# Sliding-window attention with a gated MLP on one core: the attention stages ordered in runs of two row blocks

## The chip, the core and the metric

The kernel runs on one core of a Trainium2 chip. The metric is the device time of one execution, in microseconds. A core has five engines that run their own programs and meet at semaphores: TensorE (PE in the profile; matmuls into PSUM), VectorE (DVE), ScalarE (ACT), GpSimd (POOL) and SyncE (SP, which here only issues DMAs). DMAs can be issued from SP, ACT and POOL; POOL's are listed in the profile as "software_dynamic", the others as "hardware_dynamic".

## What is computed

The reference, cut to what matters. S = 2048 rows, D = 640, 32 heads of 192, the last W = 512 keys of the cache, F = 1536:

```python
xn = layernorm(x)
q = (xn @ wq) per head
scores = q @ k[last 512].T * 192 ** -0.5
p = softmax(scores)
s = (p @ v[last 512], heads side by side) @ wo
h = sigmoid(xn @ w_gate) * (xn @ w_up)
g = silu(h @ w_down)
return x + s * g
```

## The kernel before

The program is in two parts. The first (lines 175 to 362) normalises x, turns it (`xnT`, and `xnS` with its partition halves swapped) and computes the gate `g` for all rows, which goes to DRAM as `gB_d`. It also loads the first head group's keys, values and query weights from POOL's queue and has SP turn the keys by DMA transposes (`turn_k`).

The second part is the attention, from line 365 on. Heads are taken in pairs, two pairs make a group (G = 2), so there are NG = 8 groups. Rows are taken in NST = 4 blocks of 512, of four tiles of 128. A block `n` is one (group, row block); there are 32, all four row blocks of a group after each other. For each block TensorE has four kinds of stage:

- `stage_q` (L409), three per block, the query projection: 20 matmuls on halves of the array, listed as 64*128 in the profile. DVE copies the result to `qT` (L414).
- `stage_s` (L425), eight per block, the scores: 12 matmuls of the form 64*128. ACT takes the exponential into `E` (L429).
- `stage_pv` (L441), four per block, the product with the values: 16 matmuls on the whole array (128*128). DVE takes the reciprocal of the row sums and writes `o_st` (L447, L448); after every second one SP turns `o_st` into `oT` by a DMA transpose (L454).
- `stage_wo` (L486), four per block, one per tile of 128 rows, the output projection: 12 matmuls of the form 128*128 on the `oT` of both head pairs. DVE adds it to `acc` (L525); the first group copies it (L523).

The order is written out by hand. In block n all scores come first, with the query stages of block n + 1 between them (SSQ SSQ SSQ SS). Then each of the four value stages is followed by an output stage of block n - 1. Every stage takes the next of four PSUM bank pairs (`bank2`), so a stage starts when the reader of the stage four before it is done. Each engine executes its own instructions in program order.

Weights, keys and values of the next group are loaded while this one is worked on. `load_ahead` issues them from ACT's queue: query weights and keys of one head pair in each of the group's first two blocks, values in the third (with the key transposes on SP), output weights `wo_g` in the last. The query weights, turned keys, values and output weights have two buffers each. `o_st` has two tiles.

In group 6 `prep_last` multiplies `acc` by the gate and adds x, on POOL, tile by tile, with POOL loading gate and x. In group 7 `finish` multiplies the projection by the gate on DVE (L496) and adds `acc`: on DVE, but for the last two blocks on POOL (L497). SP sends the tile out (L498). `load_gate` (L459) issues the gate loads from POOL.

Of the kernel before, what the change touches and what calls it, by code (L numbers as in the profile page):

```python
# [9 lines left out]
ALU = mybir.AluOpType  # L10
BF16 = mybir.dt.bfloat16
F32 = mybir.dt.float32
# [3 lines left out]
def kernel(  # L16
# [13 lines left out]
    nc = tc.nc  # L30
    P = 128
# [4 lines left out]
    S, D = xf.shape  # L36
# [8 lines left out]
    KC = W // P  # L45
    assert S % 512 == 0
    NST = S // 512
    TQ = 4
# [5 lines left out]
    G = 2  # L54
    NG = NPAIR // G
    NWARM = (9, 2)
    FA = 3
    PC = 3
# [29 lines left out]
    gB_d = dram.tile([S, D], BF16, name="gB_d")  # L88

    rs = dict(side="right")  # L90
    xnt_pool = ctx.enter_context(tc.tile_pool(name="xnt_pool", bufs=1, **rs))
    wq_pool = ctx.enter_context(tc.tile_pool(name="wq_pool", bufs=2, **rs))
    k_pool = ctx.enter_context(tc.tile_pool(name="k_pool", bufs=2, **rs))
    kt_pool = ctx.enter_context(tc.tile_pool(name="kt_pool", bufs=2 * G, **rs))
    v_pool = ctx.enter_context(tc.tile_pool(name="v_pool", bufs=1, **rs))

    HF = 64
# [3 lines left out]
    xnS = [xnt_pool.tile([P, NCD, 512], BF16, name=f"xnS{s}") for s in range(NST)]  # L101
    xnT = [xnt_pool.tile([P, NCD, 512], BF16, name=f"xnT{s}") for s in range(NST)]

    NV = 4 * G
    v_tiles = []
    for i in range(NV):
        vt = v_pool.tile([P, KC, DH + 2], BF16, name=f"v_sb{i}")
# [7 lines left out]

    k_of = {}

    def load_k(hp, eng):

        k_sb = k_pool.tile([P, KC * PC, 2, HF], BF16, name="k_sb")  # L120
        for i in range(2):
            hk = (2 * hp + i) // rep
            eng.dma_start(
                k_sb[:, :, i, :],
                A_k_cache[0, hk, Sk - W:Sk, :].rearrange("(p k) (j e) -> p (k j) e", k=KC, j=PC),
            )
        k_of[hp] = k_sb

    def load_v(hp, eng):
        v_t[hp] = []  # L130
        for i in range(2):
            hk = (2 * hp + i) // rep
            vt = v_tiles[(2 * hp + i) % NV]
            eng.dma_start(
                vt[:, :, 0:DH],
                A_v_cache[0, hk, Sk - W:Sk, :].rearrange("(p j) d -> p j d", j=KC),
            )
            v_t[hp].append(vt)

    def load_wq(hp, eng):  # L140


        if hp % G == 0:
            wq_t[hp // G] = wq_pool.tile([P, G * PC // 2, NCD * 2, 2, HF], BF16, name="wqp")
        wqp = wq_t[hp // G]
        for j in range(PC):
            jj = (hp % G) * PC + j
            r = HI if jj % 2 else LO
            for i in range(2):
                d0 = (2 * hp + i) * DH + j * HF  # L150
                eng.dma_start(
                    wqp[r, jj // 2, :, i, :],
                    wq_r[:, :, :, d0:d0 + HF].rearrange("p c h n -> p (c h) n"),
                )

    def turn_k(hp):
        kT = kt_pool.tile([P, KC * PC, P], BF16, name="kT")
        nc.sync.dma_start_transpose(kT[:], k_of[hp][:].rearrange("p k i e -> p (k i e)"))
        kT_t[hp] = kT


    with ExitStack() as bctx:
# [147 lines left out]
        for s in range(NST):  # L310
# [40 lines left out]
            nc.sync.dma_start(xnS[s][HI], xnT[s][LO])  # L351
            if s == 0:
                for hp in range(G):
                    load_k(hp, nc.gpsimd)
                for hp in range(G):
                    load_v(hp, nc.gpsimd)
                    load_wq(hp, nc.gpsimd)
            elif s == 1:
                for hp in range(G):
                    turn_k(hp)  # L360


    acc_pool = ctx.enter_context(tc.tile_pool(name="acc_pool", bufs=1))
    wo_pool = ctx.enter_context(tc.tile_pool(name="wo_pool", bufs=2))
    qT_pool = ctx.enter_context(tc.tile_pool(name="qT_pool", bufs=2))
    e_pool = ctx.enter_context(tc.tile_pool(name="e_pool", bufs=2))
    ost_pool = ctx.enter_context(tc.tile_pool(name="ost_pool", bufs=2))
    oT_pool = ctx.enter_context(tc.tile_pool(name="oT_pool", bufs=2 * G))
    small = ctx.enter_context(tc.tile_pool(name="small", bufs=8))
    fin = ctx.enter_context(tc.tile_pool(name="fin", bufs=2))  # L370
    fout = ctx.enter_context(tc.tile_pool(name="fout", bufs=4))
    gate_pool = ctx.enter_context(tc.tile_pool(name="gate_pool", bufs=TQ + 1))

    acc = [acc_pool.tile([P, D], F32, name=f"acc{t}") for t in range(NST * TQ)]
    wo_t = {}

    def load_wo(g, eng):
        wo_g = wo_pool.tile([P, G * PC, D], BF16, name="wo_g")
        eng.dma_start(wo_g[:], wo_r[:, g * G * PC:(g + 1) * G * PC, :])
        wo_t[g] = wo_g  # L380

    def load_ahead(g, s):


        if s < G:
            load_wq(g * G + s, nc.scalar)
            load_k(g * G + s, nc.scalar)
        elif s == G:
            for hp in range(g * G, (g + 1) * G):
                load_v(hp, nc.scalar)  # L390
                turn_k(hp)
        if s == NST - 1:
            load_wo(g, nc.scalar)

# [2 lines left out]
    def stage_q(n, u):  # L399

        g, s = blocks[n]
        if u == 0:
            qT_t[n] = qT_pool.tile([P, G * PC, 512], BF16, name="qT")
        ps = bank2()
        for c in range(NCD):
            for h in range(2):
                for b, r in enumerate((LO, HI)):
                    x = xnT if b == h else xnS
                    nc.tensor.matmul(  # L409
                        ps[:, b, :], lhsT=wq_t[g][r, u, 2 * c + h].rearrange("p i e -> p (i e)"),  # L410
                        rhs=x[s][r, c, :],
                        start=(c == 0 and h == 0), stop=(c == NCD - 1 and h == 1),
                    )
        nc.vector.tensor_copy(qT_t[n][:, 2 * u:2 * u + 2, :], ps)  # L414
# [39 lines left out]
            nc.sync.dma_start_transpose(oT[:], o_st[:].rearrange("p q d -> p (q d)"))  # L454
            oT_t[n, pp] = oT

    def load_gate(t):
        gB_sb = gate_pool.tile([P, D], BF16, name="gBa_sb")
        nc.gpsimd.dma_start(gB_sb[:], gB_d[t * P:(t + 1) * P, :])  # L459
        return gB_sb  # L460

    prep_in = {}

    def prep_load(t):
        gB_sb = load_gate(t)
        x_sb = fin.tile([P, D], BF16, name="xa_sb")
        nc.gpsimd.dma_start(x_sb[:], xf[t * P:(t + 1) * P, :])
        prep_in[t] = gB_sb, x_sb
# [20 lines left out]
                    start=(cc == 0), stop=(cc == nn - 1),  # L489
                )  # L490

    def finish(ps, gB_sb, t, d0, d1, add):
        t_sb = fin.tile([P, D], F32, name="t_sb")
        o_sb = fout.tile([P, D], BF16, name="o_sb")
        d = slice(d0, d1)
        nc.vector.tensor_tensor(t_sb[:, d], ps, gB_sb[:, d], ALU.mult)  # L496
        add.tensor_tensor(o_sb[:, d], t_sb[:, d], acc[t][:, d], ALU.add)  # L497
        nc.sync.dma_start(of[t * P:(t + 1) * P, d], o_sb[:, d])  # L498

    gates = {}  # L500

    def stage_wo(n, q):
        g, s = blocks[n]
        t = s * TQ + q
        if g == NG - 1:

            for tt in range(t, min(t + 4, NST * TQ)):
                if tt not in gates:
                    gates[tt] = load_gate(tt)
            gB_sb = gates[t]  # L510
        if n == last and q == TQ - 1:

            ps, h = bank2(), D // 2
            for i in range(2):
                wo_mm(ps[:, i, :], n, q, [(i * h, h)], i * h)
                finish(ps[:, i, 0:h], gB_sb, t, i * h, (i + 1) * h, nc.vector)
            return
        oA = flat(bank2())
        wo_mm(oA, n, q, d_chunks)
        if g == NG - 1:  # L520
            finish(oA[:, 0:D], gB_sb, t, 0, D, nc.gpsimd if n >= last - 1 else nc.vector)
        elif g == 0:
            nc.vector.tensor_copy(acc[t][:], oA[:, 0:D])  # L523
        else:
            nc.vector.tensor_tensor(acc[t][:], oA[:, 0:D], acc[t][:], ALU.add)  # L525
        if g == NG - 2:
            prep_last(t)

    blocks = [(g, s) for g in range(NG) for s in range(NST)]
    last = len(blocks) - 1  # L530
    qT_t, E_t, oT_t, ost_t = {}, {}, {}, {}
    load_wo(0, nc.gpsimd)
    for u in range(G * PC // 2):
        stage_q(0, u)
    for n, (g, s) in enumerate(blocks):

        todo = [(pp, c) for pp in range(G) for c in range(KC)]
        for k, (pp, c) in enumerate(todo):
            stage_s(n, pp, c)
            if k % 2 == 1 and k // 2 < G * PC // 2 and n < last:  # L540
                stage_q(n + 1, k // 2)
        if g + 1 < NG:
            load_ahead(g + 1, s)

        pv = [(n, pp, i) for pp in range(G) for i in range(2)]
        wo = [(n - 1, q) for q in range(TQ)] if n > 0 else []
        if n < last:
            for k, u in enumerate(pv):
                stage_pv(*u)
                if wo:  # L550
                    stage_wo(*wo[k])
        else:
            for k, u in enumerate(pv):
                stage_pv(*u)
                if k == 1:
                    stage_wo(*wo.pop(0))
            for u in wo:
                stage_wo(*u)
    for q in range(TQ):
        stage_wo(last, q)  # L560

# [28 lines left out]
```

The softmax here doesn't subtract the row's maximum and nothing guards it: scores larger than these inputs give would overflow.

## Time and profile before

| | us |
|---|---|
| median of 5 runs (lowest, highest) | 937.99 (937.67, 938.34) |
| the profiled execution | 937.75 |
| its span, first to last instruction | 936.0 |
| start of the first value stage (L441) | 182.89 |
| last matmul starts | 927.3 |

The mean granted TensorE clock is 0.997. The page shows busy time by engine, groups of instructions with their mean duration, and what ended the idle time before them. Lines of it that bear on the order of the work:

```profile
L429 ACT ACTIVATE E<-ps_all 128x1024 bf16<-128x1024 f32 x256 | 247.8, 1022 | 496.2 <-PE ps_all L425 443.6
L486 PE MATMUL ps_all<-wo_g,oT 128*128 128x512 bf16 (+2 forms) x1536 | 228.2, 299 | 0.0
L441 PE MATMUL ps_all<-v_sb,E 128*128 128x193 bf16 x2048 | 194.6, 247 | 0.1
L448 DVE TENSOR_TENSOR o_st<-ps_all,rden 128x768 bf16<-128x768 f32 x128 | 122.5, 957 | 4.9 <-DVE rden L447 0.5
```

Columns: line, engine, operation, output and inputs with their shapes, count; busy time in us and mean duration in ns; idle time of the engine just before such instructions, and what ended most of it. ACT's 496 us of idle time before exponentials is time in which TensorE works on the other stages: it costs nothing, as ACT is not the bottleneck. The mean duration of a matmul is longer than its share of the engine's time, since matmuls overlap in the array; the distance between starts is what counts.

The DMA issues of the attention, with the median time from issue to landing:

```profile
wqp<-in_A_wq_dram ACTq DMA_DIRECT2D x84, 80.0 KB, 3.0
wo_g<-in_A_wo_dram ACTq DMA_DIRECT2D x7, 960.0 KB, 5.1
k_sb<-in_A_k_cache_dram ACTq DMA_DIRECT2D x28, 192.0 KB, 4.8
v_sb<-in_A_v_cache_dram ACTq DMA_DIRECT2D x28, 192.0 KB, 3.5
```
```profile
oT<-o_st SPq DMA_TRANSPOSE x64, 3.8
wqp<-in_A_wq_dram POOLq DMA_DIRECT2D x12, 80.0 KB, 4.1
wo_g<-in_A_wo_dram POOLq DMA_DIRECT2D x1, 960.0 KB, 5.5
k_sb<-in_A_k_cache_dram POOLq DMA_DIRECT2D x4, 192.0 KB, 4.6
v_sb<-in_A_v_cache_dram POOLq DMA_DIRECT2D x4, 192.0 KB, 4.4
```

The rows of ACT's queue are the loads ahead; those of POOL's are the first group's, and the transposes of `oT` are SP's.

### The profile page before, as it was taken

The page shows a single profiled execution, that of the slowest core. Times are in us where ns is not written, and L with a number is a line of the kernel's source. Part 1 is how long each engine was busy: PE and PEld are TensorE (multiplying, and loading weights), DVE is VectorE, ACT ScalarE, POOL GpSimd, SP SyncE. Part 2 cuts the span into 40 slices and gives each one's busy share as a digit, 9 for nine tenths or more (in the row PEclk, how much of TensorE's full clock was granted, in tenths as well). Part 3 has the DMA queues.
Part 4 walks back from the last instruction along what each step waited for, and adds up shares of the span by engine and source line. Part 5 has one row for each costly group of instructions (what it writes and reads, how often), then busy time and mean ns, then how long its engine had stood idle before and what let it go on. Part 6 is the DMA issues. An engine that isn't in the chain of part 4 may idle for free.

```text
span 936.0 us, 18269 instructions
## 1 busy us (share of the span) xinstructions
PE 925.1 (99%) x8025; PEld 539.7 (58%) x8025; DVE 446.9 (48%) x636; ACT 303.8 (32%) x340; POOL 107.0 (11%) x130
## 2 busy tenths in 40 slices
PE   8999999999999999999999999999999999999996
PEld 5545445565555656555565555556555556666664
DVE  5443532454444444444444444444444444444654
ACT  4333322433333333333333333333333333333340
POOL 0070000100000000000000000000000006666005
PEclk9999999999999999999999999999999999999998
DMA  9566130385334523453347324632563348554434
GB/s 289 147 124 118 20 94 15 98 113 104 77 60 70 112 73 54 76 111 77 54 70 123 75 48 71 112 63 70 70 105 69 77 73 162 125 133 97 91 84 119
DMA packets 270144, 87.18 MB, mean 93 GB/s; under 512 B 250288, under 2 KB 266736, under 8 KB 270064
## 3 DMA queue, kind: packets, MB, share of 16 engines
q1 hardware_dynamic: 146864, 47.20, 25.8%
q10 hardware_dynamic: 118832, 24.78, 13.9%
q0 software_dynamic: 4368, 14.03, 5.6%
q8 instruction: 63, 1.03, 0.4%
q14 instruction: 17, 0.14, 0.0%
HBM read 44.70 MB, written 5.24 MB: 53 GB/s over the span
## 4 chain that ended last, share of the span: by engine, by line
PE 97%; issue 1%; POOL 1%; DMA 0%; DVE 0%; ACT 0%; SPq 0%; DVEq 0%; ACTq 0%; POOLq 0%
PE ps_all L409 22%; PE ps_all L486 21%; PE ps_all L441 19%; PE ps_all L425 18%; PE ps_all L319 10%; PE ps_all L339 6%; PE ps_all L260 1%; DMA x_sb<-in_A_x_dram 0%; POOL o_sb L497 0%; ACT E L429 0%; DVE t_sb L496 0%; POOL gBa_sb L459 0%; DVE stats L222 0%; SPq L175 0%; ACT xnT L275 0%
## 5 line engine op out<-in xcount | busy, mean ns | idle before, releaser
L429 ACT ACTIVATE E<-ps_all 128x1024 bf16<-128x1024 f32 x256 | 247.8, 1022 | 496.2 <-PE ps_all L425 443.6
L486 PE MATMUL ps_all<-wo_g,oT 128*128 128x512 bf16 (+2 forms) x1536 | 228.2, 299 | 0.0
L414 DVE CAST qT<-ps_all 128x1024 bf16<-128x1024 f32 x96 | 117.6, 1225 | 226.3 <-PE ps_all L409 226.3
L409 PE MATMUL ps_all<-xnT,wqp 64*128 64x512 bf16 x960 | 222.6, 376 | 0.0
L409 PE MATMUL ps_all<-xnS,wqp 64*128 64x512 bf16 x960 | 222.0, 376 | 0.0
L441 PE MATMUL ps_all<-v_sb,E 128*128 128x193 bf16 x2048 | 194.6, 247 | 0.1
L425 PE MATMUL ps_all<-qT,kT 64*128 64x512 bf16 x1536 | 186.7, 376 | 0.0
L441 PEld LDWEIGHTS <-E 128*128 128x128 bf16 x2048 | 171.0, 98 | 24.4 <-issue 13.6
L486 PEld LDWEIGHTS <-oT 128*128 128x128 bf16 x1536 | 121.4, 97 | 76.2
L409 PEld LDWEIGHTS <-wqp 64*128 64x128 bf16 x1920 | 93.4, 94 | 113.8 <-issue 0.3
L425 PEld LDWEIGHTS <-kT 64*128 64x128 bf16 x1536 | 72.3, 94 | 91.8 <-issue 8.4
L448 DVE TENSOR_TENSOR o_st<-ps_all,rden 128x768 bf16<-128x768 f32 x128 | 122.5, 957 | 4.9 <-DVE rden L447 0.5
L525 DVE TENSOR_TENSOR acc<-ps_all,acc 128x640 f32<-128x640 f32 x96 | 79.2, 825 | 41.7 <-PE ps_all L486 41.7
L477 POOL TENSOR_TENSOR acc<-acc,gBa_sb 128x640 f32<-128x640 f32 x16 | 22.5, 1408 | 627.6 <-DVE acc L525 627.4
L447 DVE RECIPROCAL rden<-ps_all 128x4 f32<-128x4 f32 x128 | 23.3, 182 | 98.9 <-PE ps_all L441 98.7
L325 DVE TENSOR_TENSOR hT_sb<-ps_all,sig_sb 128x512 bf16<-128x512 f32 x48 | 33.1, 692 | 50.9 <-PE ps_all L319 41.0
L319 PE MATMUL ps_all<-xnT,wg_sb 128*128 128x512 bf16 x225 | 55.9, 379 | 0.0
L319 PE MATMUL ps_all<-xnT,wu_sb 128*128 128x512 bf16 x225 | 55.9, 379 | 0.0
L339 PE MATMUL ps_all<-wd_sb,hT_sb 128*128 128x512 bf16 (+1 forms) x384 | 52.8, 299 | 0.0
L324 ACT ACTIVATE sig_sb<-ps_all 128x512 bf16<-128x512 f32 x48 | 28.6, 597 | 56.6 <-PE ps_all L319 56.2
L339 PEld LDWEIGHTS <-hT_sb 128*128 128x128 bf16 x384 | 29.7, 98 | 23.1
L319 PEld LDWEIGHTS <-wu_sb 128*128 128x128 bf16 x225 | 22.0, 98 | 26.5
(50 smaller groups left out, 237.3 us busy)
## 6 DMA issues: line engine op xcount, KB each, us to landing
wqp<-in_A_wq_dram ACTq DMA_DIRECT2D x84, 80.0 KB, 3.0
wo_g<-in_A_wo_dram ACTq DMA_DIRECT2D x7, 960.0 KB, 5.1
k_sb<-in_A_k_cache_dram ACTq DMA_DIRECT2D x28, 192.0 KB, 4.8
v_sb<-in_A_v_cache_dram ACTq DMA_DIRECT2D x28, 192.0 KB, 3.5
gBa_sb<-gB_d POOLq DMA_DIRECT2D x32, 160.0 KB, 2.9
gB_d<-gB_sb POOLq DMA_DIRECT2D x16, 160.0 KB, 2.6
xnS<-xnT SPq DMA_DIRECT2D x8, 320.0 KB, 4.7
xa_sb<-in_A_x_dram POOLq DMA_DIRECT2D x16, 160.0 KB, 3.4
```

The costliest lines, as they stand in the source:

```text
L319: nc.tensor.matmul(gu[:, i, :], lhsT=w[:, c, f * P:(f + 1) * P], rhs=xnT[s][:, c, :], start=(c == 0), stop=(c == NCD - 1),)
L324: nc.scalar.activation(sig_sb[:], gu[:, 0, :], AF.Sigmoid)
L325: nc.vector.tensor_tensor(hT_sb[:, f, :], gu[:, 1, :], sig_sb[:], ALU.mult)
L339: nc.tensor.matmul(oB_ps[:, d0:d0 + dsz], lhsT=hT_sb[:, f, q * P:(q + 1) * P], rhs=wd_sb[:, f, d0:d0 + dsz], start=(f == 0), stop=(f == NF ...
L409: nc.tensor.matmul(ps[:, b, :], lhsT=wq_t[g][r, u, 2 * c + h].rearrange("p i e -> p (i e)"), rhs=x[s][r, c, :], start=(c == 0 and h == 0), ...
L414: nc.vector.tensor_copy(qT_t[n][:, 2 * u:2 * u + 2, :], ps)
L425: nc.tensor.matmul(ps[:, b, :], lhsT=kT[r, c * PC + j, :], rhs=qT[r, pp * PC + j, :], start=(j == 0), stop=(j == PC - 1),)
L429: nc.scalar.activation(E_t[n, pp][:, c, :, :], ps, AF.Exp, scale=scale_qk)
L441: nc.tensor.matmul(o_ps[:, q // 2, q % 2, 0:DH + 1], lhsT=E[:, c, i, q * P:(q + 1) * P], rhs=vt[:, c, 0:DH + 1], start=(c == 0), stop=(c = ...
L448: nc.vector.tensor_tensor(o_st[:, :, i * DH:(i + 1) * DH].rearrange("p (b i) d -> p b i d", b=2), o_ps[:, :, :, 0:DH], rden[:].to_broadcas ...
L486: nc.tensor.matmul(oA[:, d0 - base:d0 - base + dsz], lhsT=oT_t[n, pp][:, q * PC + j, :], rhs=wo_t[g][:, cc, d0:d0 + dsz], start=(cc == 0), ...
L525: nc.vector.tensor_tensor(acc[t][:], oA[:, 0:D], acc[t][:], ALU.add)
```

## The change

Blocks are joined to runs of two (row blocks 0 and 1, then 2 and 3, of a group); the last two blocks of all stay single. There are 17 runs. In a run all scores of its blocks come first, 16 in a full run, with the query stages of the next run spread between them; then all its value stages, with the output stages of the run before spread between them: none in the first run, one after each value stage in the full ones, two after each in the run of block 30.

The query weights, turned keys, values and output weights have one buffer each instead of two. `qT`, `E` and `oT` have more. All their loads are issued from POOL's queue instead of ACT's: in a group's first run the next group's query weights and keys after the scores, and this group's output weights after the value stages; in its second run the key transposes (SP) after the scores and the next group's values after the value stages. POOL executes `prep_last` of group 6 in the same queue.

The gate loads of the last group move from POOL's queue to ACT's, and all final additions to DVE; the product with the gate is written back into PSUM and read from there.

```diff
-    wq_pool = ctx.enter_context(tc.tile_pool(name="wq_pool", bufs=2, **rs))
+    wq_pool = ctx.enter_context(tc.tile_pool(name="wq_pool", bufs=1, **rs))
...
-    kt_pool = ctx.enter_context(tc.tile_pool(name="kt_pool", bufs=2 * G, **rs))
+    kt_pool = ctx.enter_context(tc.tile_pool(name="kt_pool", bufs=G, **rs))
...
-    NV = 4 * G
+    NV = 2 * G
...
-    wo_pool = ctx.enter_context(tc.tile_pool(name="wo_pool", bufs=2))
-    qT_pool = ctx.enter_context(tc.tile_pool(name="qT_pool", bufs=2))
-    e_pool = ctx.enter_context(tc.tile_pool(name="e_pool", bufs=2))
+    wo_pool = ctx.enter_context(tc.tile_pool(name="wo_pool", bufs=1))
+    qT_pool = ctx.enter_context(tc.tile_pool(name="qT_pool", bufs=4))
+    e_pool = ctx.enter_context(tc.tile_pool(name="e_pool", bufs=2 * G))
     ost_pool = ctx.enter_context(tc.tile_pool(name="ost_pool", bufs=2))
-    oT_pool = ctx.enter_context(tc.tile_pool(name="oT_pool", bufs=2 * G))
+    oT_pool = ctx.enter_context(tc.tile_pool(name="oT_pool", bufs=3 * G))
...
-    fout = ctx.enter_context(tc.tile_pool(name="fout", bufs=4))
-    gate_pool = ctx.enter_context(tc.tile_pool(name="gate_pool", bufs=TQ + 1))
+    fout = ctx.enter_context(tc.tile_pool(name="fout", bufs=3))
+    gate_pool = ctx.enter_context(tc.tile_pool(name="gate_pool", bufs=TQ + 2))
...
-    def finish(ps, gB_sb, t, d0, d1, add):
-        t_sb = fin.tile([P, D], F32, name="t_sb")
+    def finish(ps, gB_sb, t, d0, d1):
         o_sb = fout.tile([P, D], BF16, name="o_sb")
         d = slice(d0, d1)
-        nc.vector.tensor_tensor(t_sb[:, d], ps, gB_sb[:, d], ALU.mult)
-        add.tensor_tensor(o_sb[:, d], t_sb[:, d], acc[t][:, d], ALU.add)
+        nc.vector.tensor_tensor(ps, ps, gB_sb[:, d], ALU.mult)
+        nc.vector.tensor_tensor(o_sb[:, d], ps, acc[t][:, d], ALU.add)
         nc.sync.dma_start(of[t * P:(t + 1) * P, d], o_sb[:, d])
...
+    runs = [[n, n + 1] for n in range(0, last - 1, 2)] + [[last - 1], [last]]
     qT_t, E_t, oT_t, ost_t = {}, {}, {}, {}
-    load_wo(0, nc.gpsimd)
-    for u in range(G * PC // 2):
-        stage_q(0, u)
-    for n, (g, s) in enumerate(blocks):
...
+    load_wo(0)
+    for n in runs[0]:
+        for u in range(G * PC // 2):
+            stage_q(n, u)
+    for r, ns in enumerate(runs):
+        g = blocks[ns[0]][0]
+        at_start, at_end = blocks[ns[0]][1] == 0, blocks[ns[-1]][1] == NST - 1
+        before = runs[r - 1] if r > 0 else []
+
+        s_list = [(n, pp, c) for n in ns for pp in range(G) for c in range(KC)]
+        q_list = [(n, u) for n in sum(runs[r + 1:r + 2], []) for u in range(G * PC // 2)]
+        done = 0
+        for k, x in enumerate(s_list):
+            stage_s(*x)
+            if done < len(q_list) and (k + 1) * (len(q_list) + 1) >= (done + 1) * len(s_list):
+                stage_q(*q_list[done])
+                done += 1
+        for u in q_list[done:]:
+            stage_q(*u)
+
+        hps = range((g + 1) * G, (g + 2) * G) if g + 1 < NG else []
+        if at_start:
+            for hp in hps:
+                load_wq(hp)
+                load_k(hp)
+        if at_end:
+            for hp in hps:
+                turn_k(hp)
+        for n in before + (ns if r == len(runs) - 1 else []):
+            if blocks[n][0] == NG - 1:
+                for t in range(blocks[n][1] * TQ, blocks[n][1] * TQ + TQ):
+                    gates[t] = load_gate(t, nc.scalar)
+
+        pv_list = [(n, pp, i) for n in ns for pp in range(G) for i in range(2)]
+        wo_list = [(n, q) for n in before for q in range(TQ)]
+        done = 0
+        for k, x in enumerate(pv_list):
+            stage_pv(*x)
+            share = (k + 1) * len(wo_list) // len(pv_list)
+            if r == len(runs) - 1:
+                share = (k + 1) // 2 if k + 1 < len(pv_list) else len(wo_list)
+            while done < share:
+                stage_wo(*wo_list[done])
+                done += 1
+        if at_start and g > 0:
+            load_wo(g)
+        if at_end:
+            for hp in hps:
+                load_v(hp)
     for q in range(TQ):
         stage_wo(last, q)
```

## The prediction

> **What bounds the kernel now.** I read the engine table first, then the TensorE timeline of one steady block, then POOL's timeline near the end and the last DVE rows, then the landings of the DMA transposes. The engine table of the page:
>
> ```profile
> PE 925.1 (99%) x8025; PEld 539.7 (58%) x8025; DVE 446.9 (48%) x636; ACT 303.8 (32%) x340; POOL 107.0 (11%) x130
> ```
>
> TensorE has no idle time to give; the change can save only what its instructions cost, and any wait that it puts on TensorE is paid in full. The timeline of one block (start, duration, engine, line):
>
> ```profile
> 505.13 1.46 PE L425 MATMUL ps_all<-qT,kT 64*128 64x512 bf16 x12
> ...
> 508.59 1.46 PE L425 MATMUL ps_all<-qT,kT 64*128 64x512 bf16 x12
> 509.98 1.53 PE L441 MATMUL ps_all<-v_sb,E 128*128 128x193 bf16 x16
> 511.35 1.79 PE L486 MATMUL ps_all<-wo_g,oT 128*128 128x512 bf16 x12
> 512.98 1.52 PE L441 MATMUL ps_all<-v_sb,E 128*128 128x193 bf16 x16
> ...
> 520.32 1.79 PE L486 MATMUL ps_all<-wo_g,oT 128*128 128x512 bf16 x12
> 522.04 1.47 PE L425 MATMUL ps_all<-qT,kT 64*128 64x512 bf16 x12
> ```
>
> Starts, not durations, give the pace, since matmuls overlap. Two score stages and one query stage (SSQ) take 3.455 us (505.13 to 508.59); two score stages alone are six pairs of 0.2155 = 1.29, one query stage 2.16; a value stage 1.37 (509.98 to 511.35), an output stage 1.63, both 2.99. The values of the block eleven further on start at 772.09: a block takes (772.09 - 509.98) / 11 = 23.83.
>
> **Part 1, fewer mode turns.** The column 64*128 or 128*128 is the array's mode. From scores to values: 508.59 + 1.29 = 509.88, but 509.98 is seen, 0.10 late. From output to scores: 520.32 + 1.63 = 521.95, seen 522.04, 0.09 late. The first SSQ after it takes 3.47 (the next scores start at 525.51), 0.015 more. Together 0.205 us a block; the rest adds up (3 x 3.455 + 1.29 + 4 x 2.99 = 23.62, a block 23.83). Before there are 32 turns one way and 31 back. After there are 17 runs, so 17 and 16. Fifteen of each go: 15 x 0.205 = **-3.1 us**. No matmul is added or dropped. The new order inside a phase (SSSQ SSQ SSQ SSSQ SSQ SSQ SS) asks more of ACT in places: three S take 1.94 on TensorE and 2.9 on ACT (Exp 1.02, pitch 0.97), but the Q of 2.16 behind them lets ACT catch up before the ring of four PSUM pairs comes round. Nothing there.
>
> **Part 2, loads on POOL and single buffers.** Each load now waits on POOL for TensorE to finish with the old tile. The wq load of the next group waits for the last query stage of the group's first run (1.3 us before the values start at T), and 4 K loads share its queue: 12 x 0.73 + 4 x 1.03 = 12.9 us of issue, last landing by T + 16. Its user comes with the next query stage, T + 26. Queued behind it stand the wo load and then V, each with a 23 us phase before its use and 5 us to land. The K transposes wait on SP for the last score stage, ahead of the first oT transpose by 5.9 us, with 1.9 us each of issue. All covered, ten times 5 us or more. What ACT is rid of cost nothing either: its 6 to 7 us of issue fell in a phase where it idles. Two places are not covered.
>
> *The first run.* It has eight value stages and no output stages between them, so o_st tiles (two buffers) come every 2.7 us instead of every 6. The third may be written only when the first transpose has landed. Before, only four value stages stand there, and nobody waits. These are the rows of the first two transposes of before (SP's timeline, one each), the first value stage starting at 182.89, then the landings of both from the answer on tile oT in that window:
>
> ```profile
> 182.89 5.62 PE L441 MATMUL ps_all<-v_sb,E 128*128 128x193 bf16 x64
> 188.44 0.82 PE L425 MATMUL ps_all<-qT,kT 64*128 64x512 bf16 x6
> ```
> ```profile
> 187.06 1.49 SPq L454 DMA_TRANSPOSE oT<-o_st  x1
> ```
> ```profile
> 189.82 1.28 SPq L454 DMA_TRANSPOSE oT<-o_st  x1
> ```
> ```profile
> DMA to landing us min/median/max: 6.1/6.5/6.8
> ```
>
> Over the whole run the same answer gives 3.6/3.8/6.8: these two are the slow ones, issued amid wq and K loads, as the new ones will be. With T the first value stage: a stage every 1.36, so scores resume at T + 11.0 and, three scores later, a query stage at T + 12.9 wants the pair of the eighth value stage. The second transpose starts at T + 6.93; after it lands, two o_st writes and a reciprocal (0.96 + 0.18 + 0.96 and gaps: 2.2) must pass DVE. Stall = 6.93 + L + 2.2 - 12.9 = L - 3.8. Queued behind the waiting write on DVE are the reciprocals and writes of the later stages, for whose PSUM TensorE waits. At L = 3.8 it is 0, at 6.8 it is 3.0. I take 6.8, **+3.0**, as the row nearest in place and load; bounds 0 (TensorE waits for nothing there before, so no gain) and, from rival 2, 5.5.
>
> *The last wo load.* POOL adds gate and x into acc for 16 tiles. Its rows:
>
> ```profile
> 776.20 1.40 POOL L477 TENSOR_TENSOR acc<-acc,gBa_sb 128x640 f32<-128x640 f32 x1 [603.37 <-DVE acc L525]
> 777.68 1.40 POOL L478 TENSOR_TENSOR acc<-acc,xa_sb 128x640 f32<-128x640 f32 x1
> 779.03 0.58 POOL L459 DMA_DIRECT2D gBa_sb<-gB_d  x1
> 779.60 0.54 POOL L467 DMA_DIRECT2D xa_sb<-in_A_x_dram  x1
> 780.16 1.41 POOL L477 TENSOR_TENSOR acc<-acc,gBa_sb 128x640 f32<-128x640 f32 x1
> ```
>
> One tile takes 3.96 us of POOL (2.83 without loads), an output stage comes every 2.99. Before, four tiles are followed by a 12 us pause and POOL catches up; after, eight come in a row, and load_wo for the last group stands behind the second eight in POOL's program. T being the start of that run's values (772.09 for 776.20, so 4.1 to the first tile): 4.1 + 8 x 2.83 + 6 x 1.13 = T + 33.5. The one wo load that POOL issues in before lands in 5.5: T + 39.0. TensorE reaches its first use after 8 x 2.99, a one-block score phase of 11.66, turns of 0.2 and a value stage of 1.37: T + 37.1. **+1.9**; by the seven ACT loads of the same size (5.0 to 6.4) 1.4 to 2.8. V of the last group stands behind the first eight (4.1 + 31.7 + 3.0, landing 4.4 later: 43.2 us after that run's values begin) and is needed at 47.5.
>
> **Part 3, the end.** The gates now come on ACT: the first six are free when the exponentials are done, the seventh and eighth wait for the first two output tiles, with the last block's exponentials queued behind them, a dozen us ahead of need. The last additions move from POOL to DVE. Near the end DVE waited for POOL:
>
> ```profile
> 928.02 0.49 DVE L496 TENSOR_TENSOR t_sb<-ps_all,gBa_sb 128x320 f32<-128x320 f32 x1 [0.66 <-POOL o_sb L497]
> ```
>
> The first of the last seven tiles starts at 917.86 in before and DVE ends at 930.76. Where DVE does both operations in before, they start 0.91 and 0.75 apart: 6 x 1.66 + 2 x 1.0 from 917.86 is 929.8, -0.9. Writing the product back into PSUM has no row; with 0.91 for both it is +0.1. I take **-0.5**. TensorE ends at 927.6 and hides the earlier ones. In the run before that, two finishes and a value stage take DVE 4.5 for 4.62 of TensorE: covered, barely.
>
> **Sum.** -3.1 + 3.0 + 1.9 - 0.5 = +1.3: span 936.0 to 937.3. The profiled execution took 937.75 (span and 1.75 around it), the median of the runs is 937.99, so 939.3.
>
> [...] In the profiled window of 50 to 66 us, where POOL issued 2.56 MB of such loads, the DMA engines were busy 90.2%; while ACT issued six wq loads (183 to 187) 43.3%. On the page, POOL's queue moved 14.03 MB in 4368 packets (3.2 KB each), SP's 47.20 MB in 146864 (321 B). [...] No row here has both queues together. TensorE's granted clock is 1.00 from 20 to 920 us, without a gap. [...]
>
> **Rivals.** (1) *Faster: the transposes land as usual.* POOL's DMAs leave gaps and L stays near 3.8: stall 0; wo at 1.6 and the end at -0.8 give -2.3, 935.7. For it: 64 transposes have a median of 3.8. Against it: both that were issued at this place took over 6. (2) *Slower: the transposes starve.* The second lands only when the last K load has, issued by T + 11.6 and 4.6 later (POOL's K row): T + 16.2, L = 9.3, stall 5.5, sum +3.8, **941.8**. It is slower by my bound from L = 7.4. For it: the 90% above, and loads that go on twice as long as before; against it: two transposes in 183 to 197 kept landing beside 128-byte loads. (3) *The turns save nothing:* the 0.2 belongs to something that each block still pays. Then +4.4, 942.4. Against it: the delay stands exactly at both turns.
>
> **How the numbers follow.** Forecast 0.48, rival 1 0.12, rival 2 0.33, rival 3 0.05, the rest 0.02. A difference of 0.2% (1.9 us) is what measurements of this kernel can tell from none; the forecast is inside it, rival 1 below, rivals 2 and 3 above. With the rest split: faster 0.13, same 0.48, slower 0.39. The known bounds give 935.4 (0, 1.4, -0.9) to 940.8 (3.0, 2.8, +0.1); with most of rival 2 the range is 936.0 to 942.6, the forecast's own 937.0 to 939.9.
>
> **What would show it.** After: steady runs of two blocks should be 47.45 long (2 x 23.83 - 0.2). TensorE should wait about 3 us in the scores after the first run's values, with DVE's o_st writes released by oT landings of some 6.8; and 1.9 us once, before the first L486-type matmul of the last group, with POOL's wo load issued 33.5 after the run's values begin. DVE alone should end the kernel. If wq arrives late in any run, or steady runs are longer than 47.7, the prediction is wrong in its base.

## The result, and the profile after

| | before | after |
|---|---|---|
| median of the runs | 937.98 us (41 runs) | 940.6 us (21 runs) |
| lowest, highest | 937.56, 938.39 | 936.42, 944.65 |
| ratio after / before | | 1.0027, 95% interval 1.0018 to 1.0036 |
| the profiled execution, its span | 937.75, 936.0 | 938.06, 936.3 |

The changed kernel is slower by 0.27%, just over what can be told from no change. Its executions spread over 8.2 us where those of before lie within 0.8. The profiled one is 2.5 us below the median, so its own sum comes first and the spread after it.

The engine table of after:

```profile
PE 923.9 (99%) x8025; PEld 546.9 (58%) x8025; DVE 450.6 (48%) x639; ACT 302.2 (32%) x340; POOL 203.3 (22%) x254
```

TensorE still has 99%, but POOL's work has nearly doubled (107.0 before): it now issues all loads of weights, keys and values. The table of busy time hides what moved; the waits of TensorE show it (engine, tile and line, what it waited for, sum, times, longest):

```profile
PE ps_all L412 <- DVE o_st L435: 2.4, 1, 2.4
PE ps_all L473 <- DMA wo_g<-in_A_wo_dram: 1.9, 1, 1.9
```

The two long waits outside the prologue stand at the two places that the prediction named. Before has neither.

**The first run.** Its first value stage starts at 201.13. DVE's timeline behind it:

```profile
210.99 0.96 DVE L435 TENSOR_TENSOR o_st<-ps_all,rden 128x768 bf16<-128x768 f32 x1 [2.66 <-DMA oT<-o_st]
211.86 0.17 DVE L434 RECIPROCAL rden<-ps_all 128x4 f32<-128x4 f32 x1
212.07 0.96 DVE L435 TENSOR_TENSOR o_st<-ps_all,rden 128x768 bf16<-128x768 f32 x1
212.94 0.17 DVE L434 RECIPROCAL rden<-ps_all 128x4 f32<-128x4 f32 x1
215.32 0.96 DVE L435 TENSOR_TENSOR o_st<-ps_all,rden 128x768 bf16<-128x768 f32 x1 [2.21 <-DMA oT<-o_st]
```

The answer on tile `oT` for the first two transposes:

```profile
DMA to landing us min/median/max: 5.6/6.4/7.2
```

TensorE's timeline, score rows at that place:

```profile
212.12 1.78 PE L412 MATMUL ps_all<-qT,kT 64*128 64x512 bf16 x12
...
216.33 0.82 PE L412 MATMUL ps_all<-qT,kT 64*128 64x512 bf16 x6 [2.43 <-DVE o_st L435]
```

The chain reads backwards: TensorE's scores wait for a PSUM pair, the pair for DVE's `o_st` write, the write for the transpose that still reads that tile. The second transpose took 7.18 us; the prediction's L - 3.8 (L is that landing time) gives 3.4, and the three gaps of TensorE there add up to 3.3 over their usual pace.

Something else stands beside it, in the table by stretch (start and end, length, busy time and instructions of each engine, granted clock, DMA share, GB/s):

```profile
core 0: us, PE busy (x) PEld busy (x) DVE busy (x) ACT busy (x) POOL busy (x), PEclk, DMA share, GB/s
213.60:216.30 2.70, 0.30 (x4) 0.00 (x0) 0.98 (x2) 1.37 (x2) 0.00 (x0) 1.00 1.21 192
217.10:220.40 3.30, 3.04 (x17) 1.67 (x16) 0.26 (x1) 1.02 (x1) 0.00 (x0) 0.50 1.38 184
220.50:224.00 3.50, 3.50 (x36) 2.40 (x34) 1.23 (x1) 1.94 (x2) 0.00 (x0) 1.00 0.34 75
```

Right after the wait TensorE runs at half clock for 3.413 us: 17 matmuls in 3.3 us, then 36 in 3.5. From the first run's values to the next run's it is 39.29; the third experiment, which has no wait there, takes 34.40. Of these 4.89 us 3.3 are the wait; the rest, some 1.55, is put down to the half clock.

**The last `wo` load.** POOL's timeline from the last full run on, whose values start at 850.70, then TensorE's in the run of block 30:

```profile
854.88 1.39 POOL L464 TENSOR_TENSOR acc<-acc,gBa_sb 128x640 f32<-128x640 f32 x1 [6.36 <-DVE acc L506]
...
882.98 1.40 POOL L465 TENSOR_TENSOR acc<-acc,xa_sb 128x640 f32<-128x640 f32 x1
884.32 0.88 POOL L379 DMA_DIRECT2D wo_g<-in_A_wo_dram  x1
```
```profile
886.49 1.53 PE L428 MATMUL ps_all<-v_sb,E 128*128 128x193 bf16 x16
889.90 0.38 PE L473 MATMUL ps_all<-wo_g,oT 128*128 128x512 bf16 x1 [1.88 <-DMA wo_g<-in_A_wo_dram]
```

The load is issued 33.6 us after that run's values begin and lands 5.45 later. The output stage would start 1.37 after 886.49; it starts 2.04 later than that.

**The end.** From the last block's value stages to the end of the span it is 27.02 us in before and 23.52 in after. The rows of the end of the program show why (engine's queue, durations in ns as least/median/most, first and last start). Before, then after:

```profile
L585 POOLq DRAIN  x3: 40/93/7802, 927.4 to 935.7; - x3
L585 SPq DRAIN  x3: 7/7/7, 932.8 to 935.5; - x3
```
```profile
L591 POOLq DRAIN  x3: 40/102/5952, 884.2 to 935.9; - x3
L591 SPq DRAIN  x3: 7/7/12, 935.4 to 935.7; - x3
```

In before, POOL's drain began at 927.4 and took 7.8 us, to 935.2, while SP's outputs were through at 932.8. POOL's last addition had ended here:

```profile
924.95 4.52 POOL L497 TENSOR_TENSOR o_sb<-t_sb,acc 128x640 bf16<-128x640 f32 x3
```

So the kernel before ended with some 2.4 us in which only POOL's drain was under way, 5.7 us behind its last addition (929.47). In after POOL's long drain lies at 884, and the end follows the last output's landing (935.21). The other 1.0 us of the 3.5 is DVE, whose last row starts 20.34 us after the last values began, against 21.31 in before. The two rows, before, then after:

```profile
930.27 0.49 DVE L497 TENSOR_TENSOR o_sb<-t_sb,acc 128x320 bf16<-128x320 f32 x1
933.11 0.49 DVE L483 TENSOR_TENSOR o_sb<-ps_all,acc 128x320 bf16<-128x320 f32 x1
```

**The sum of the profiled execution.** Twelve full runs in a row are 47.44 each, against 2 x 23.83: 15 turns, -3.2. First run: +3.3 of wait, +1.55 of half clock. `wo`: +2.04. End: -3.5. Together +0.2; the spans differ by +0.3.

### The profile page after: what moved, and what is told of

Read it like the earlier page. It is cut to its first block, busy times and chain, and to the rows that moved or that the text cites. A ratio compares the mean times of both kernels' runs of the same rounds, so it can differ in the third digit from the quotient of the medians.

```text
span 936.3 us, 18269 instructions
## 1 busy us (share of the span) xinstructions
PE 923.9 (99%) x8025; PEld 546.9 (58%) x8025; DVE 450.6 (48%) x639; ACT 302.2 (32%) x340; POOL 203.3 (22%) x254
## 5 line engine op out<-in xcount | busy, mean ns | idle before, releaser
L412 PE MATMUL ps_all<-qT,kT 64*128 64x512 bf16 x1536 | 184.3, 376 | 2.6 <-DVE o_st L435 2.4
L396 PEld LDWEIGHTS <-wqp 64*128 64x128 bf16 x1920 | 97.0, 94 | 112.2 <-issue 2.1
L412 PEld LDWEIGHTS <-kT 64*128 64x128 bf16 x1536 | 75.6, 94 | 92.3 <-issue 7.6
L151 POOL DMA_DIRECT2D wqp<-in_A_wq_dram x96 | 69.0, 737 | 168.0 <-PE ps_all L396 144.4
L134 POOL DMA_DIRECT2D v_sb<-in_A_v_cache_dram x32 | 24.1, 754 | 261.3 <-PE ps_all L428 261.3
```

The costliest lines, as they stand in the source:

```text
L151: nc.gpsimd.dma_start(wqp[r, jj // 2, :, i, :], wq_r[:, :, :, d0:d0 + HF].rearrange("p c h n -> p (c h) n"),)
L396: nc.tensor.matmul(ps[:, b, :], lhsT=wq_t[g][r, u, 2 * c + h].rearrange("p i e -> p (i e)"), rhs=x[s][r, c, :], start=(c == 0 and h == 0), ...
L412: nc.tensor.matmul(ps[:, b, :], lhsT=kT[r, c * PC + j, :], rhs=qT[r, pp * PC + j, :], start=(j == 0), stop=(j == PC - 1),)
```

## The experiments

The theory by now: the wait of the first run (with the clock behind it) and the late `wo` load are the whole loss, the turns and POOL's early end the whole gain. Rivals: other loads of POOL, the in-place product or the longer runs cost something too; the end gained for another reason.

### 1. Three o_st tiles

```diff
-    ost_pool = ctx.enter_context(tc.tile_pool(name="ost_pool", bufs=2))
-    oT_pool = ctx.enter_context(tc.tile_pool(name="oT_pool", bufs=3 * G))
+    ost_pool = ctx.enter_context(tc.tile_pool(name="ost_pool", bufs=3))
+    oT_pool = ctx.enter_context(tc.tile_pool(name="oT_pool", bufs=2 * G + 1))
```

> The changed kernel with three o_st tiles instead of two (and five oT tiles instead of six, to fit). Theory A: the third value-stage pair of the first run no longer waits for a transpose; of the 3.3 us that TensorE lost there at most 0.6 stay, and the half-clock window of 3.4 us behind it (1.5 us) is gone. The wait for the last wo load (2.0 us) stays. Median near 934 instead of 940.6, and a spread of the executions well under the 8 us of the changed kernel if the first run's wait is what takes the clock down. Theory B (the loads from POOL disturb every run, and that is what the executions differ by): at most 2 us off the median, spread still 5 us or more.

Measured: 935.15 us (934.68 to 935.79, 6 runs), ratio to before 0.9969 [0.9957, 0.998]. The first interval is 34.40, without a wait, although the transposes landed after 6.3 and 11.1 us; the spread shrank from 8.2 to 1.1 us. Most of the spread goes with the first run's wait. The `wo` wait stayed, a little longer, with a half clock behind it (TensorE's waits, then the stretches at and after it):

```profile
PE ps_all L473 <- DMA wo_g<-in_A_wo_dram: 2.6, 1, 2.6
```
```profile
882.90:885.50 2.60, 0.09 (x2) 0.00 (x0) 1.14 (x2) 0.00 (x0) 0.00 (x0) 1.00 1.01 360
886.20:889.50 3.30, 3.30 (x14) 1.52 (x12) 0.98 (x2) 0.00 (x0) 0.00 (x0) 0.50 0.24 85
```

The load took 6.1 us here. In this execution 2.7 + 1.7 us instead of 2.0 is lost at this place, which is why the gain fell short of the 934 expected.

### 2. The last wo load on ACT's queue

```diff
-        nc.gpsimd.dma_start(wo_g[:], wo_r[:, g * G * PC:(g + 1) * G * PC, :])
+        eng = nc.scalar if g == NG - 1 else nc.gpsimd
+        eng.dma_start(wo_g[:], wo_r[:, g * G * PC:(g + 1) * G * PC, :])
```

> The changed kernel with the last group's wo load issued from ACT instead of behind POOL's sixteen tiles. Theory A: the wait of 2.0 us before the first output stage of the last group goes, nothing else; median near 938.6, and the spread of several us stays, since the first run's wait is still there. If instead the wait for wo is what takes the clock down in some executions, the spread falls to about 1 us. Theory B: spread unchanged, median down by 2.

Measured: 937.59 (936.39 to 940.24, 11 runs), 0.9998 [0.9989, 1.0006]. The `wo` wait is gone (from the start of block 30's values to that of the last block's it is 24.24, where after has 26.28). The first run's wait is there, and a spread of 3.9 us: more than without that wait, but half of the 8.2 of after. The median is 1.0 below the 938.6 expected, and no profile shows why.

### 3. Both

The two edits above together.

> Both of these together. Theory A: median near 932 (span 936.3 less 3.3, 1.5 and 2.0, plus up to 0.6 left of the first wait, and 1.75 around it), executions within 1 us of each other, granted clock as in the kernel before. Theory B: median 936 or more with a spread of several us.

Measured: 930.71 (930.56 to 931.05, 5 runs), 0.9922 [0.9909, 0.9934]. TensorE's waits and the cores' line:

```profile
PE ps_all L248 <- DVE warm L243: 1.3, 1, 1.3
PE ps_all L260 <- ACT xnT L275: 0.2, 1, 0.2
```
```profile
core 0: 928.8 us, clock 1.000
```

Only the prologue's waits are left, no stretch is at half clock, and the spread is 0.5 us. The expectation was 932, with up to 0.6 of the first wait left; nothing of it is. This version is 0.8% faster than before and 9.9 us faster than after. It says that nothing else in the change costs anything large: -3.2 and -3.5 make 931.3 of before's 937.98, 0.6 above what is measured.

### 4. Runs of one block, on top of both

```diff
-    wq_pool = ctx.enter_context(tc.tile_pool(name="wq_pool", bufs=1, **rs))
+    wq_pool = ctx.enter_context(tc.tile_pool(name="wq_pool", bufs=2, **rs))
...
-    qT_pool = ctx.enter_context(tc.tile_pool(name="qT_pool", bufs=4))
-    e_pool = ctx.enter_context(tc.tile_pool(name="e_pool", bufs=2 * G))
+    qT_pool = ctx.enter_context(tc.tile_pool(name="qT_pool", bufs=2))
+    e_pool = ctx.enter_context(tc.tile_pool(name="e_pool", bufs=2))
...
-    runs = [[n, n + 1] for n in range(0, last - 1, 2)] + [[last - 1], [last]]
+    runs = [[n] for n in range(last + 1)]
```

> The kernel with both of these, but in runs of one block: 63 turns of the array's mode instead of 33 (query weights doubled again, E and qT with two buffers, as the order needs). Theory A: thirty turns at 0.10 us cost 3.1 us: median 3 us above the one with runs of two, near 934.5. If the turns cost nothing (the third rival of the prediction) it is the same time or less.

Measured: 934.2 (933.69 to 934.55, 5 runs), 0.9958 [0.9944, 0.9971]: 3.5 above the third experiment, with blocks of 23.83 as in before. The turns cost what the starts of before said; the third rival (they save nothing) falls. The profiles of the two are 3.8 apart (spans of 932.5 and 928.8), of which 0.5 is a prologue that happened to be longer (the first query matmul starts at 164.88 and 164.34); the other 3.2 are fifteen turns each way at 0.21 the pair. What is left against before, 3.9 us by the medians of that chip, is the end (3.5) and little else.

### 5. No loads in the first run

On top of the second experiment, with two `o_st` tiles. The kernel leaves out the loads of the second group's query weights and keys and uses the first group's again, so part of its output is another computation.

```diff
             for hp in hps:
+                if hp < 2 * G:
+                    wq_t[1] = wq_t[0]
+                    k_of[hp] = k_of[hp - G]
+                    continue
                 load_wq(hp)
```

> The kernel with the wo load on ACT and o_st and oT as in the changed kernel, but the second head group's query weights and keys are not loaded: it uses the first group's again, so that part of the output is another computation. Theory A (the first run's transposes are slow because these loads pass through the DMA engines beside them): the first two oT transposes land in 3.6 to 3.9 us instead of 5.6 to 7.2, TensorE waits at most 0.1 us after the first run's values, the clock stays up, median near 931. Rival (the transposes are slow at this place by themselves, being the first, or because o_st tiles come every 2.7 us): landings of 5 us or more and a wait of 2 us or more remain.

Measured: 931.0 (930.88 to 931.1, 4 runs), 0.9926 [0.9911, 0.994], 6.6 below the second experiment. The landings of the first two transposes, with the loads (second experiment), then without (fifth):

```profile
DMA to landing us min/median/max: 6.0/7.2/8.5
```
```profile
DMA to landing us min/median/max: 3.6/3.6/3.6
```

At 3.6 nobody waits (the first interval is 34.40), and the clock stays up (mean 0.999): the loads beside the transposes, and not the number of `o_st` tiles alone, make the wait.

### 6 and 7. The same loads on ACT's queue

On top of the second experiment; the wq and K loads of group 1 alone:

```diff
     def load_k(hp):
+        eng = nc.scalar if G <= hp < 2 * G else nc.gpsimd
...
-            nc.gpsimd.dma_start(
+            eng.dma_start(
```

(and the same in `load_wq`). Both experiments have this kernel: one execution, then six. What is asked is why the first run's two transposes land late: in 6.0 and 8.5 us in the second experiment, in 3.6 each in the fifth.

> The same kernel with the second group's query weights and keys loaded, but from ACT's queue instead of POOL's. [...] If it is the bytes and not the queue, they land in 6 to 7 us as in the kernel before, and TensorE waits 2 to 3.5 us there; ACT's exponentials of the second run may come 1 to 2 us late behind 13 us of issue.

> The kernel with the second group's loads on ACT's queue again, one more look and timed. If POOL's packets slow the transposes beyond what the bytes do, the second transpose lands in 6 to 7 us again (with POOL's queue it took 7.2 to 9.4 in five looks with two o_st tiles) and the median is 2 us or more below 937.6, the time with POOL's loads and the same wo load. If the first look was chance, it lands in 7.2 to 9.4.

Measured: 934.94 in the one execution; 935.21 (934.49 to 935.65, 6 runs), 0.997 [0.9958, 0.9982] in the six, 2.4 below the second experiment. The landings in the profile of the latter:

```profile
DMA to landing us min/median/max: 5.2/5.7/6.1
```

The second transposes took 6.5 and 6.1 us, the waits were 2.6 and 2.3, and neither profile has a stretch at half clock after it (mean clocks of 0.999 and 1.000). With POOL issuing the same bytes and two `o_st` tiles, five profiles (after, the second experiment and the three below) have the second landing at 7.2, 8.5, 9.0, 9.4 and 8.7. So beside the loads on ACT's queue the landing is 2.5 to 2.9 us over 3.6, and with POOL's queue it is another 1 to 3 more. The queue is not the only difference: POOL issued the sixteen loads from 0.9 us before the first value stage to 11 us after it, ACT from 0.3 to 17 us after it, so fewer of them stood beside the second transpose.

The first run's interval is 38.31 and 37.92 here, 3.9 and 3.5 over the third experiment's, of which the waits for `o_st` make only 2.6 and 2.3. The other 1.2 is ACT's: its exponentials came only when the loads had been issued. In the first of the two profiles TensorE's scores resumed at 212.15, and ACT's row is

```profile
218.46 4.69 ACT L419 ACTIVATE E<-ps_all 128x1024 bf16<-128x1024 f32 x5 [15.90 <-DMA wqp<-in_A_wq_dram]
```

This is the price of that cure; the third experiment, with a third `o_st` tile, has no such wait.

### 8. A late addition on POOL

On top of the third, one column of the last tile added on POOL after that tile's first half, as in before's end:

```diff
+        if t == NST * TQ - 1 and d0 == 0:
+            nc.vector.tensor_copy(acc[t][:, 1:2], acc[t][:, 1:2])
...
+                if i == 0:
+                    z = small.tile([P, 2, 2, 1], F32, name="rden")
+                    nc.gpsimd.tensor_tensor(z[:, 0, 0, :], acc[t][:, 0:1], acc[t][:, 1:2], ALU.add)
```

> The kernel with both repairs, plus one addition of a single column on POOL close to the end (it waits for DVE's work on the last tile and nothing waits for it; a one-column copy on DVE orders it). Theory A (after POOL's last work its drain takes 5.7 us, 929.5 to 935.2 in the kernel before, and that held the end): the program ends about 2.5 us later, 933.2 instead of 930.7. Rival (what the kernel before waits for at the end is the DMAs that POOL issued late): no difference, under 0.5 us.

Measured: 931.77 (931.55 to 931.95, 4 runs), 0.9934 [0.9919, 0.9949], 1.06 above the third. The rows of the end of the program:

```profile
L597 POOLq DRAIN  x3: 40/93/4079, 925.2 to 929.8; - x3
L597 SPq DRAIN  x3: 7/7/7, 928.3 to 929.6; - x3
```

One column on POOL, and its drain ends at 929.3 (925.2 + 4.1), 0.9 after SP's outputs were through at 928.4: this is the added 1.06. The 2.5 expected was too much, since the small addition ended at 925.5 and the drain ended 3.9 behind it instead of 5.7 as in before. That late arithmetic on POOL holds the end is shown; how much of before's 2.4 it is, is read from before's rows.

### 9. Late gate loads on POOL's queue

On top of the third:

```diff
-                    gates[t] = load_gate(t, nc.scalar)
+                    gates[t] = load_gate(t, nc.gpsimd)
```

> The kernel with both repairs, with the last group's gate loads back on POOL's queue, so that its last DMAs stand in the tail but no arithmetic. Theory A (drain after POOL's arithmetic): within 0.5 us of 930.7, as the last gate load is issued when the second to last tile's neighbours are done, some 7 us before the end. Rival (late POOL DMAs hold the end): 1.5 us or more later.

Measured: 931.01 (930.67 to 932.03, 4 runs), 0.9929 [0.9913, 0.9946], no difference to the third that its spread would show. The rows of the end of the program:

```profile
L592 POOLq DRAIN  x3: 40/102/4457, 915.5 to 928.6; - x3
L592 SPq DRAIN  x3: 7/7/13, 928.1 to 928.4; - x3
```

This tests the rival less than was meant. The last gate load was issued at 915.57, 13 us before the end and not 7, and POOL's drain behind it ended at 920.0, 8 us before SP's outputs were through. That DMA issues of POOL at that place cost nothing is shown; that later ones would not is not. Against the rival in before itself stand before's own times: its last gate load was issued at 924.37 and landed at 927.23, 8 us before the drain ended, and the eighth experiment moved the end with arithmetic alone.

### 10 to 12. The changed kernel profiled three more times

No edit.

> The changed kernel itself, one more look. Theory A: span = 928.8 (both waits repaired) + the first run's wait (the second transpose's landing less 3.8) + the wait for wo (2 to 3 us) + about 1.5 us for each half-clock window of 3.4 us that stands behind one of the waits; within 0.7 us. Rival: time is lost elsewhere too (steady runs longer than 47.5, other waits on TensorE).

> The same, another look: the sum of the same four terms within 0.7 us, whatever the time is.

> The same, a third look: the sum of the same four terms within 0.7 us, whatever the time is.

Measured: 940.05, 940.45 and 940.3 us, spans of 938.3, 938.7 and 938.5: around the median, as the first profile was not.

| us | after | again 1 | again 2 | again 3 |
|---|---|---|---|---|
| landing of the second transpose | 7.18 | 8.95 | 9.38 | 8.66 |
| first run's values to the next run's (34.40 without wait) | 39.29 | 41.01 | 41.83 | 41.02 |
| half clock | 3.413 | 3.413 | 6.827 | 3.413 |
| block 30's values to the last block's (24.24 without wait) | 26.28 | 26.54 | 26.38 | 26.59 |
| a full run | 47.44 | 47.44 | 47.44 | 47.44 |
| last values to end | 23.52 | 23.52 | 23.53 | 23.52 |

What varies between these four profiles sits in the two places and in the start of the first values. The expectation asked that the span follow from the landing and the half-clock windows within 0.7 us: this held for the first (0.5 too short), and missed in the others, 0.8 too long in the second and 1.0 too short in the third. In the third the values began 0.6 later than in the third experiment, which a formula of the two places can't know. In the second the clock stayed low for two windows, during the wait and after it; beyond the wait both together cost 1.8 us:

```profile
213.70:218.20 4.50, 0.24 (x4) 0.00 (x0) 0.93 (x2) 1.29 (x2) 0.00 (x0) 0.77 1.13 123
216.20:222.90 6.70, 4.61 (x22) 1.94 (x23) 2.00 (x3) 1.02 (x1) 0.00 (x0) 0.50 1.23 162
```

With these the median can be added up: -3.2 for the turns, +5.1 for the wait (landing 8.9), +1.5 for the clock, +2.3 for `wo`, -3.5 for the end: +2.2. On 937.98 this is 940.2, where 940.6 is measured.

No execution above 940.5 was profiled, so what the slowest ones (to 944.65) lose is not shown. The mean clock recorded for each execution of after points the same way: 0.998 in the fastest, 0.993 in the slowest. A half-clock stretch of 3.413 us takes an estimated 0.0018 off that mean, so the slowest would have some three of them.

## Why the prediction was right, and where it was wrong

The forecast was 939.3, within 0.2% of before. The median is 940.6: inside the stated range of 936.0 to 942.6, but above the forecast's own 937.0 to 939.9, and with 2.6 us over before on the slower side, which had a chance of 0.39 against 0.48 for no difference.

- **Part 1, the turns: right.** 47.45 was predicted for a full run, 47.44 is seen in every kernel with runs of two; the return to one block costs 3.5.
- **Part 2, the first run: the mechanism right, the size too small.** The wait stands where it was put, by way of `o_st` and DVE, and L - 3.8 gives it to 0.1 in the profile of after. The step that failed is "I take 6.8": that row had ACT's loads beside it. With ACT's queue the landing is indeed 6.1 and 6.5; with POOL's it is 7.2 to 9.4. At the median the wait is 5.1, between the 3.0 taken and rival 2's 5.5. Rival 2 was thus near in size, but its picture, a landing only with the last K load, is contradicted in all five profiles: in that of after the second transpose lands 14.1 after the first value stage and the last K load 17.4 after it, in the second repetition 16.3 and 19.6, and it is 3.3 to 3.5 apart in the others too. Its number came near because the K loads landed 6.7 us after issue in after and not 4.6. The prediction also says "No row here has both queues together", which is a misreading: in group 6 of before POOL's loads of gate and x (160 KB each) stand beside `oT` transposes, which landed in 3.7 to 5.1 us there.
- **Part 2, the clock: not in the sum.** Before's clock of 1.00 from 20 to 920 us was read where TensorE did not wait (busy 899.88 us of the 900), and the sum took its waits of 3.0 and 1.9 at full clock. A stretch at half clock stood behind the first run's wait in all five profiles that had it beside POOL's loads (3.413 us, in the second repetition 6.827), and once behind the `wo` load, in the first experiment. Taking the wait (L - 3.8) out, 1.4 to 1.8 us was paid behind each, in the second repetition for both stretches together. Six other waits had none behind them. The length of the wait alone does not tell them apart: 2.6 us stood before a half clock in the first experiment, and 2.6 us, in two pieces, before none in the sixth.
- **Part 2, the last wo load: right.** Issue at +33.5 predicted, +33.6 seen; +1.9 predicted, 2.0 to 2.4 seen (2.7 in the first experiment).
- **Part 2, "needed at T + 26": wrong for the first run, at no cost.** Without output stages the next query stage comes at T + 12.9 there. In after the wait for `o_st` held it back to T + 16.3, and the last wq load had landed at T + 15.1. In the first and third experiments it did start at T + 12.9, with the last wq loads landing at T + 19.5 and T + 17.7; they came in time for the parts that use them, and no wait on them is seen.
- **Part 3, the end: DVE alone ends the kernel, as predicted, but the term is mis-sized: -0.5 against -3.5.** DVE's share is -1.0, since the product written back into PSUM cost no more than into the buffer (0.82 to 0.83 us for 128x640, starts 0.92 and 0.74 apart). The rest was not in the sum at all: the prediction read DVE's last rows and its waits for POOL, and not POOL's drain behind them.
- **The net.** The end was priced 3.0 too dear and the turns 0.1, the clock 1.5, the landing 2.1 and `wo` 0.4 too cheap. They add up to +0.9 of the 1.3 us by which the median missed, so the forecast came out near partly by luck.
- **Rival 1** (landings of 3.8) falls: that needs the loads gone, as in the fifth experiment. **Rival 3** falls by the fourth.

What stays open: why a transpose lands later beside the loads on POOL's queue than beside the same loads on ACT's. No run separated the two queues' packets, and packet sizes and the pace of issue differ between them too: the loads on POOL's queue beside the first run of after moved 1.77 MB in 832 packets (2.1 KB each), those on ACT's queue at that place in before 0.89 MB in 7040 (126 B each). The fourth experiment prices the boundary between the phases; that it is the array's mode that costs there, and not something else at the same boundary, was not tested apart. And the drain of before is 1.9 us longer behind its last addition than that of the eighth experiment, for no reason that a run shows.

## What to carry to other kernels

Where stages are gathered into longer runs, count the buffers that were paced by the stages between them: here one more `o_st` tile was worth 5.5 us of 940, and the change lost its gain for the lack of it. Read the program's end down to the drains, and ask which engine's last arithmetic the end waits for, before costing an edit there. Price a wait on TensorE of two or three microseconds with the clock behind it: here it added 1.4 to 1.8 us behind six such places and nothing behind six others.

## What the runs showed of the hardware that was not expected

**Half clock behind 2.15 us of idle time and more.** The edges of the half-clock stretches give a grid of 3.413 us in each profile (in after they stand at 217.05 and 220.47, and the next at 933.86, 209 times 3.413 later); in experiments 6 and 7, which have none before the end, the ends of the full-clock stretch do (925.01 us, 271 windows, in both). Idle time of TensorE in each window of that grid that has more than 1 us of it, between the prologue and the end, and whether the next window was at half clock:

```
profile        window from   idle us   next window
experiment 2   214.10        3.02      half
again 1        215.32        2.80      half
experiment 1   882.72        2.56      half
again 2        212.73        2.46      half
after          213.64        2.43      half
again 3        215.88        2.40      half
again 2        216.14        2.15      half
again 3        212.46        1.80      full
experiment 6   211.98        1.78      full
again 3        888.30        1.76      full
experiment 7   212.14        1.71      full
again 2        888.57        1.67      full
again 1        211.90        1.47      full
after          886.06        1.45      full
again 1        887.74        1.39      full
```

The line lies between 1.8 and 2.15 us of 3.413, in these fifteen windows. A wait that the grid cuts in two can pass without it: the `wo` wait of after had 1.45 us of its 1.9 in one window. The 2.6 of the first experiment fell into one window whole. As the grid stands elsewhere in each profile, a wait of two to three microseconds would by this reading cost some 1.6 us more in one execution than in another, an estimate from the 1.4 to 1.8 us above. The ends of matmuls are modelled in the trace, so the idle times are not exact.

**POOL's drain.** It ended 5.7 us after POOL's last addition in before and 3.9 us after it in experiment 8, and held the end of the program in both. The other kernels have it as well, far from the end, where it cost nothing: 3.4 to 3.9 us after the last addition where that is POOL's last work (experiments 2 to 7), 0.4 us after the landing of the `wo` load where that is POOL's last issue (after, its three repetitions and experiment 1), and 1.0 us after the landing of the last gate load in experiment 9.

**Landings that nobody waits for.** With three `o_st` tiles the second and third transposes of the first run landed 11.1 and 15.2 us after issue in the profile of the first experiment, and TensorE did not wait at all there: the third tile buys more than the queue takes.
